# Four shared banks in place of three and one, and the two heads' exponentials of a half pair made in the same step

## The chip, the cores and the metric

The kernel runs on one core of a Trainium2 chip. The metric is the device time of one execution in microseconds, from the program's first instruction to its last; a measurement is the median of several executions. A core has four engines that compute here: TensorE (PE in the profile, with its weight loads as PEld), VectorE (DVE), ScalarE (ACT) and GpSimd (POOL). Each works through its own instruction stream in order. SyncE (SP) issues most of the DMAs, also in order. Results of matmuls land in PSUM, which has eight banks of 2 KB a partition.

## What is computed

Linear attention with exponential features for 8 batches of 8 heads, then a mixer block over the attention's output: a token-mixing MLP and a channel-mixing MLP.

```python
def phi(x):                                   # x: (8, 8, 576, 64), w_phi: (64, 128)
    proj = einsum('bhsd,df->bhsf', x, w_phi)
    proj = proj - max(abs(proj), axis=-1)
    return concatenate([exp(proj), exp(-proj)], axis=-1)
q_p, k_p = phi(q), phi(k)
kv  = einsum('bhsf,bhsd->bhfd', k_p, v);  z = sum(k_p, axis=2)
x   = einsum('bhsf,bhfd->bhsd', q_p, kv) / (einsum('bhsf,bhf->bhs', q_p, z) + 1e-6)
x   = x.transpose(0, 2, 1, 3).reshape(8, 576, 512)
u   = x + (relu(x.T @ w_tok1) @ w_tok2).T     # w_tok1: (576, 256), w_tok2: (256, 576)
out = u + relu(u @ w_ch1) @ w_ch2             # w_ch1: (512, 1536), w_ch2: (1536, 512)
```

## The kernel before

Heads are worked on in pairs: 32 pairs, `i` from 0 to 31, four to a batch. Most products are made of three matmuls of 32-bit halves (`mm3`, line 87): a high and a low part of each operand, without the product of the two low parts.

Five Python generators write the program: `keys`, `queries`, `token_stream`, `load_weights` and `channel_stream`. `weave` advances whichever is furthest behind its share. That gives each instruction a priority. A scheduler then sets the real order of every engine, from its own estimates, and it gives a tile one of the buffers of its tag as that tag has one free. So a change of a tag or of a due step reorders all engines, and only the built order shows how.

**Keys** (line 283). For each pair `load` fetches `raw`, whose single buffer holds the keys of pair i and the queries of pair i-1; `stack` splits them (`stk`, `stq`). `less_max` (line 221) makes scores in five groups: matmuls into a bank (`ppk`), ACT copies one half out (`part`), DVE adds the other half (which frees the bank) and takes the largest magnitude, and POOL subtracts it (`pmk`). ACT makes the exponentials `kp` and `add_kv` adds to `pkv`.

**Queries** (line 350) go in pieces `(i, k, j)`: pair, half of the sequence, and half of that half's rows. `less_max` makes `ppq` and `pmq`. For pairs from 8 on, `across` sends both pieces of a half through memory and back so that they come back turned: DVE transposes into `tq`, one DMA `dq` writes it, four DMAs `qt` read it. What comes back is sorted by head, and from there `j` is the head. A piece waits in the list `waiting` with a due step; from that step on `turn` (line 420) makes that head's exponentials, two signs each: ACT writes `qf` and `qh`, then DVE (first sign) or POOL (second sign) writes `ql = qf - qh`. Each of the tags `qf`, `qh` and `ql` has two buffers, one for each sign, so the exponentials of the next piece can only be written when the matmuls of the one before have read theirs. A one-column copy by POOL (line 445) that the next `qh` begins with shows that moment: POOL waits there for PE. `numerators` (line 504) makes the six matmuls `pn` of one head; ACT and DVE empty that bank and DVE and POOL divide.

**Token mixing** (line 541) begins when a half batch is attended: transposes `px`, a split into `xh` and `xl`, matmuls into `pa`, a relu split into `ah` and `al`, matmuls into `ph`, and DVE's addition to `xt` (line 586). For batch 0 its banks are those of the tags `a0` and `a1`, later those of `rest`.

**Channel mixing** (line 590) takes 18 blocks of 256 tokens, `channel_mix(i)`. It alternates six up-projections, `h{i}_0` to `h{i}_5` of 24 matmuls each, with down-projections `acc`. All `h` share one bank (except in the last three blocks, where odd ones take another), so the next up-projection begins when ACT has written `gh` and DVE `gl` from the one before (lines 617 and 618). The next block begins when the batches under it have been mixed.

The eight PSUM banks: one `keys`, three `rest`, one `kv`, one `h`, and `a0` and `a1`. `rest` serves query scores, transposes, numerators and, from batch 1 on, token mixing. Lines that the change touches: 59, 233, 236, 389 and 608.

Of the kernel before, what the change touches and what calls it, by code (L numbers as in the profile page):

```python
# [8 lines left out]
F32 = mybir.dt.float32  # L9
# [8 lines left out]
P = 128  # L18
B, H, S, D = 8, 8, 576, 64
NP = H // 2  # L20
F = 128
# [14 lines left out]
BEHIND = 2  # L36
TURNED = 4
CH = 256
# [9 lines left out]
def mixer_kernel(ctx, tc, qk, vm, vt, w_phi, w1, w2, wc1, wc2d, out):  # L48
# [5 lines left out]
    ps_w = ctx.enter_context(tc.tile_pool(name="ps_w", bufs=1, space=PSUM))  # L54
# [1 line left out]
    ps_h = ctx.enter_context(tc.tile_pool(name="ps_h", bufs=1, space=PSUM))  # L56
    ps_a = ctx.enter_context(tc.tile_pool(name="ps_a", bufs=1, space=PSUM))

    REST = dict(tag="rest", bufs=3)

    def streamed(pool, shape, dtype, **kw):

# [158 lines left out]
    def less_max(ts, units, name, base=None, early=False):  # L221

        n, kind = len(units), name[0]
        if early and base == D:
            ps = ps_a.tile([P, 2, 2, F], F32, tag=f"a{nplain['k'] % 2}", name=f"pp{name}")
            nplain["k"] += 1
        elif early and base == 0 and (nplain["q"] % 2 == 0 or nplain["q"] >= BORROWED):
            ps = ps_h.tile([P, 2, 2, F], F32, tag="h", name=f"pp{name}")  # L230
            nplain["q"] += 1
        elif early and base == 0:
            ps = ps_w.tile([P, 2, 2, F], F32, tag="keys", name=f"pp{name}", bufs=1)
            nplain["q"] += 1
        elif kind == "k":
            ps = ps_w.tile([P, 2, 2, F], F32, tag="keys", name=f"pp{name}", bufs=1)
        else:
            ps = ps_w.tile([P, 2, 2, F], F32, name=f"pp{name}", **REST)
        for i, u in enumerate(units):
            t, c = (ts[1], 512) if u is None else (ts[u[0]], P * u[1])  # L240
            if base is None:
                nc.tensor.matmul(ps[:, i].rearrange("p two f -> p (two f)"), t[:, c:c + P],  # L242
                                 wp2.rearrange("p two f -> p (two f)"), start=True, stop=True)
            else:
                rows = slice(D, P) if name == "k0_0" else slice(0, P)
                nc.tensor.matmul(ps[:, i, 0], t[rows, c:c + P], wz[rows, base // D], start=True, stop=True)  # L246
        if base is None:
            part = wk.tile([P, 2, F], F32, tag="part", name=f"part{name}")
            nc.scalar.copy(part[:, :n], ps[:, :n, 1])
            pr = wk.tile([P, 2, F], F32, tag="p", name=f"p{name}")  # L250
            nc.vector.tensor_tensor(pr[:, :n], ps[:, :n, 0], part[:, :n], op=ALU.add)
            pr, eng = pr[:, :n], nc.gpsimd
        else:
            pr, eng = ps[:, :n, 0], nc.vector
        mx = column(wk, 2, tag=f"mx{kind}", name=f"mx{name}")
        nc.vector.tensor_reduce(mx[:, :n], pr, axis=AX.X, op=ALU.max, apply_absolute_value=True)  # L256
        pm = wk.tile([P, 2, F], F32, tag=f"pm{kind}", name=f"pm{name}", bufs=1 if kind == "t" else 2)
        eng.tensor_tensor(pm[:, :n], pr, mx[:, :n].unsqueeze(2).to_broadcast([P, n, F]), op=ALU.subtract)  # L258
        return pm
# [90 lines left out]
    def queries():  # L350
        waiting, split_up, row_major, pm = [], [], [], None
        pieces = [(i, k, j) for i in range(B * NP) for k in range(2) for j in range(2)]
        n = 0
        while n < len(pieces) or waiting or split_up or row_major:
            for done in row_major:
                flip(*done)
                yield 0.2
            row_major = []
            for work in split_up:
                yield from until(lambda: work[0] in kvs)  # L360
                if work[0] < ROWS:
                    row_major += [done for done in (row_numerators(*work),) if done]
                else:
                    numerators(*work)
                yield 0.75
            split_up = []
            while waiting and len(split_up) < 2 and (waiting[0][0] <= n or n >= len(pieces)):
                due, work = waiting.pop(0)
                split_up.append(turn(*work, pm if via(work[0]) and n < len(pieces) else None))
                yield 0.02 if via(work[0]) else 0.25  # L370
            if n < len(pieces):
                i, k, j = pieces[n]
                if (k, j) == (0, 0):
                    plain = 0 if i < PLAIN else None
                    if i < PLAIN:
                        yield from until(lambda: i in pairs)
                        ts = pairs[i]
                    else:
                        yield from until(lambda: i + 1 in raws or i + 1 == B * NP)
                        if i + 1 == B * NP:  # L380
                            load(i + 1)
                        ts = stack(raws[i + 1], 0, f"q{i}")
                    asked.add(i)
                    tail = less_max(ts, [None], f"t{i}", plain, i < NP)
                    yield 0.11
                pm = less_max(ts, [(j, 2 * k), (j, 2 * k + 1)], f"q{i}_{k}{j}", plain, i < NP)
                if via(i):
                    across(i, k, j, pm, tail)
                waiting.append((n + 1 + BEHIND * via(i), (i, k, j, pm, tail)))
                yield 0.22  # L390
            n += 1

# [2 lines left out]
    def via(i):  # L395
        return i >= ROWS and i % NP < TURNED
# [23 lines left out]
    def turn(i, k, j, pm, tail, behind):  # L420
# [3 lines left out]
        else:  # L424
            ptr = ps_w.tile([P, 3, P], F32, **REST, name=f"pt{i}_{k}{j}")
            rows = [pm[:, 0], pm[:, 1]]
# [31 lines left out]
    def row_numerators(i, k, j, qps):  # L458
# [6 lines left out]
        if j == 0:  # L465
            sums[0] = ps_w.tile([P, 2, 3, D + 1], F32, **REST, name=f"pr{i}_{k}")
        pn = sums[0]
# [122 lines left out]
    def channel_mix(i, segs):  # L590
        uh, ul = [], []
        for c in range(NC_):
            h = streamed(wk, [P, CH], F32R, tag=f"uh{c}", name=f"uh{i}_{c}", bufs=1)
# [11 lines left out]

        def up_proj(ep):
            if i >= LAST and ep % 2:
                ph = ps_w.tile([P, 2, CH], F32, tag="keys", name=f"h{i}_{ep}", bufs=1)
            else:
                ph = ps_h.tile([P, 2, CH], F32, tag="h", name=f"h{i}_{ep}")  # L610
            for k in range(2):
                es = slice((2 * ep + k) * P, (2 * ep + k + 1) * P)
                for c in range(NC_):
                    mm3(ph[:, k], (wc1_h[:, c, es], wc1_l[:, c, es]), (uh[c], ul[c]), c == 0, c == NC_ - 1)
            gh = streamed(wk, [P, 2, CH], F32R, tag="g", name=f"gh{i}_{ep}", bufs=4)
            gl = streamed(wk, [P, 2, CH], F32R, tag="g", name=f"gl{i}_{ep}", bufs=4)
            nc.scalar.activation(gh, ph, AF.Relu)  # L617
            nc.vector.scalar_tensor_tensor(gl, ph, 0.0, gh.bitcast(F32), op0=ALU.max, op1=ALU.subtract)  # L618
            return gh, gl
# [119 lines left out]
```

## Time and profile before

| | |
|---|---|
| median of 3 executions | 1119.68 us (1118.68 to 1120.17) |
| the profiled execution: its own time | 1120.8 us |
| the profiled execution: span, first to last instruction | 1119.0 us |
| TensorE busy | 1092.4 us of the span |
| TensorE weight loads busy | 1073.2 us |
| VectorE / ScalarE / GpSimd busy | 708.9 / 556.1 / 567.0 us |
| mean granted TensorE clock | 0.995 of full |

Busy time is the time in which an engine had an instruction under way. Matmuls overlap and their ends are modelled, so the time between the starts of two matmuls is the better measure of how fast PE goes. Idle time of an engine is put down to whatever ended it.

### The profile page before, as it was taken

The page shows a single profiled execution, that of the slowest core. Times are in us where ns is not written, and L with a number is a line of the kernel's source. Part 1 is how long each engine was busy: PE and PEld are TensorE (multiplying, and loading weights), DVE is VectorE, ACT ScalarE, POOL GpSimd, SP SyncE. Part 2 cuts the span into 40 slices and gives each one's busy share as a digit, 9 for nine tenths or more (in the row PEclk, how much of TensorE's full clock was granted, in tenths as well). Part 3 has the DMA queues.
Part 4 walks back from the last instruction along what each step waited for, and adds up shares of the span by engine and source line. Part 5 has one row for each costly group of instructions (what it writes and reads, how often), then busy time and mean ns, then how long its engine had stood idle before and what let it go on. Part 6 is the DMA issues. An engine that isn't in the chain of part 4 may idle for free.

```text
span 1119.0 us, 24637 instructions
## 1 busy us (share of the span) xinstructions
PE 1092.4 (98%) x9040; PEld 1073.2 (96%) x9040; DVE 708.9 (63%) x1775; ACT 556.1 (50%) x1589; POOL 567.0 (51%) x1047
## 2 busy tenths in 40 slices
PE   9999999999999999999999999999999989999998
PEld 8998999989998899999999999999999989999998
DVE  6889964467667676767666575764776776642111
ACT  4766553345546464656545464454565656441110
POOL 2334342367647665766656484663675766430110
PEclk9999999999999999999999999999999999999999
DMA  8545401133313232333323232122332232200000
GB/s 204 170 135 151 133 28 52 34 94 78 87 30 92 74 76 71 85 84 75 74 60 80 57 95 69 53 66 70 76 75 63 75 85 45 62 21 20 20 20 19
DMA packets 186744, 82.73 MB, mean 74 GB/s; under 512 B 159424, under 2 KB 171200, under 8 KB 186624
## 3 DMA queue, kind: packets, MB, share of 16 engines
q1 hardware_dynamic: 185104, 80.74, 27.9%
q8 instruction: 71, 1.16, 0.4%
q10 hardware_dynamic: 1520, 0.43, 0.2%
q14 instruction: 49, 0.40, 0.1%
HBM read 57.54 MB, written 23.59 MB: 73 GB/s over the span
## 4 chain that ended last, share of the span: by engine, by line
PE 77%; DVE 9%; POOL 4%; DMA 3%; ACT 3%; issue 2%; SPq 1%; ACTq 0%; POOLq 0%; DVEq 0%
PE h L87 24%; PE acc L87 23%; PE pkv L327 8%; PE pn L87 6%; PE ph L87 4%; PE pa L87 4%; PE pr L472 2%; PE ppk L242 2%; PE ppq L242 2%; DMA raw<-in_qk 1%; PE px L551 1%; DMA v<-in_vm 1%; PE ppq L246 1%; POOL pmq L258 1%; DMA qt<-dq 1%
## 5 line engine op out<-in xcount | busy, mean ns | idle before, releaser
L87 PE MATMUL acc<-gh,wc 128*128 128x256 f32 x1728 | 337.6, 282 | 0.0
L87 PEld LDWEIGHTS acc<-gh,wc 128*128 128x128 f32 x1728 | 273.6, 188 | 0.2
L87 PE MATMUL h<-uh,wc_h 128*128 128x256 f32 x864 | 244.1, 283 | 3.5 <-DVE gl L618 3.1
L87 PE MATMUL h<-uh,wc_l 128*128 128x256 f32 x864 | 244.1, 283 | 0.0
L87 PE MATMUL h<-ul,wc_h 128*128 128x256 f32 x864 | 242.9, 281 | 0.8 <-POOL ul L598 0.8
L87 PE MATMUL acc<-gl,wc 128*128 128x256 f32 x864 | 239.8, 281 | 0.0
L87 PEld LDWEIGHTS h<-uh,wc_h 128*128 128x128 f32 x864 | 162.5, 188 | 5.5 <-PE pn L87 2.8
L87 PEld LDWEIGHTS h<-ul,wc_h 128*128 128x128 f32 x864 | 162.7, 188 | 1.2 <-POOL ul L598 1.0
L87 PEld LDWEIGHTS acc<-gl,wc 128*128 128x128 f32 x864 | 162.5, 188 | 0.0
L87 PEld LDWEIGHTS h<-uh,wc_l 128*128 128x128 f32 x864 | 162.5, 188 | 0.0
L327 PE MATMUL pkv<-v,kp 128*128 128x65 f32 (+2 forms) x1152 | 160.2, 270 | 1.8 <-ACT kp L302 0.7
L327 PEld LDWEIGHTS pkv<-v,kp 128*128 128x128 f32 x1152 | 150.5, 192 | 3.5 <-ACT kp L302 1.6
L302 ACT ACTIVATE kp<-pmk 128x256 f32<-128x256 f32 (+1 forms) x320 | 108.5, 389 | 67.1 <-POOL pmk L258 43.9
L618 DVE SCALAR_TENSOR_TENSOR gl<-h,gh 128x512 fp32r<-128x512 f32 x108 | 73.5, 680 | 98.2 <-ACT gh L617 95.0
L447 POOL TENSOR_TENSOR ql<-qf,qh 128x320 fp32r<-128x320 f32 (+1 forms) x96 | 80.1, 834 | 72.4 <-ACT qh L446 72.1
L617 ACT ACTIVATE gh<-h 128x512 fp32r<-128x512 f32 x108 | 64.4, 596 | 101.1 <-PE h L87 99.4
L438 ACT ACTIVATE qf<-qt 128x320 f32<-128x320 f32 (+1 forms) x192 | 81.6, 437 | 63.0 <-POOL qf L437 29.0
L87 PE MATMUL pn<-qh,kv 128*128 128x320 f32 (+1 forms) x384 | 106.6, 308 | 3.8 <-ACT qh L446 1.6
L598 POOL TENSOR_TENSOR ul<-xt,uh 128x64 fp32r<-128x64 f32 (+3 forms) x120 | 60.6, 530 | 92.3 <-ACT uh L597 92.3
L446 ACT ACTIVATE qh<-qt 128x320 fp32r<-128x320 f32 (+1 forms) x192 | 82.9, 436 | 29.1 <-POOL qh L445 27.0
L217 POOL TENSOR_TENSOR stk<-raw,stk 64x512 fp32r<-64x512 f32 (+1 forms) x48 | 68.3, 1422 | 47.7 <-DVE stk L216 45.2
L258 POOL TENSOR_TENSOR pmk<-pk,mxk 128x256 f32<-128x256 f32 (+1 forms) x120 | 72.8, 606 | 36.0 <-DVE mxk L256 27.8
(129 smaller groups left out, 2293.1 us busy)
## 6 DMA issues: line engine op xcount, KB each, us to landing
raw<-in_qk SPq DMA_DIRECT2D x23, 576.0 KB, 4.2
rawc<-in_wc SPq DMA_DIRECT2D x24, 512.0 KB, 4.1
v<-in_vm SPq DMA_DIRECT2D x31, 256.0 KB, 4.1
dq<-tq SPq DMA_DIRECT2D x24, 320.0 KB, 2.1
qt<-dq SPq DMA_DIRECT2D x96, 80.0 KB, 2.9
dq<-tq SPq DMA_DIRECT2D x24, 256.0 KB, 2.0
qt<-dq SPq DMA_DIRECT2D x96, 64.0 KB, 2.9
out_x<-xt SPq DMA_DIRECT2D x12, 256.0 KB, 2.1
```

The source lines that it names most:

```text
L87: nc.tensor.matmul(o, a, m, start=first and i == 0, stop=last and i == 2, skip_group_check=group_ok)
L217: nc.gpsimd.tensor_tensor(t[lo:lo + D], src, t[base:base + D].bitcast(F32), op=ALU.subtract)
L242: nc.tensor.matmul(ps[:, i].rearrange("p two f -> p (two f)"), t[:, c:c + P], wp2.rearrange("p two f -> p (two f)"), start=True, stop=True)
L258: eng.tensor_tensor(pm[:, :n], pr, mx[:, :n].unsqueeze(2).to_broadcast([P, n, F]), op=ALU.subtract)
L302: nc.scalar.activation(kp[:, :len(us), sg], pm[:, :len(us)], AF.Exp, scale=1.0 - 2.0 * sg)
L327: nc.tensor.matmul(o, kp[:, n, sg], v, start=g == 0 and n == 0 and sg == 0, stop=u is None, skip_group_check=True)
L438: nc.scalar.activation(full, src, AF.Exp, scale=1.0 - 2.0 * sg)
L446: nc.scalar.activation(hi, src, AF.Exp, scale=1.0 - 2.0 * sg)
L447: (nc.gpsimd if sg else nc.vector).tensor_tensor(lo, full, hi.bitcast(F32), op=ALU.subtract)
L598: nc.gpsimd.tensor_tensor(l[:, d:d + n], t[:, c, o:o + n], h[:, d:d + n].bitcast(F32), op=ALU.subtract)
L617: nc.scalar.activation(gh, ph, AF.Relu)
L618: nc.vector.scalar_tensor_tensor(gl, ph, 0.0, gh.bitcast(F32), op0=ALU.max, op1=ALU.subtract)
```

## The change

The tag `keys` goes; what used it takes a buffer of `rest`, which now has four. And the due step of a turned piece depends on `j`: the second piece keeps its step, the first comes one step later, so that both are due in the same one.

```diff
-    REST = dict(tag="rest", bufs=3)
+    REST = dict(tag="rest", bufs=4)
...
         elif early and base == 0:
-            ps = ps_w.tile([P, 2, 2, F], F32, tag="keys", name=f"pp{name}", bufs=1)
+            ps = ps_w.tile([P, 2, 2, F], F32, name=f"pp{name}", **REST)
             nplain["q"] += 1
         elif kind == "k":
-            ps = ps_w.tile([P, 2, 2, F], F32, tag="keys", name=f"pp{name}", bufs=1)
+            ps = ps_w.tile([P, 2, 2, F], F32, name=f"pp{name}", **REST)
...
-                waiting.append((n + 1 + BEHIND * via(i), (i, k, j, pm, tail)))
+                waiting.append((n + 1 + (BEHIND + 1 - j) * via(i), (i, k, j, pm, tail)))
...
             if i >= LAST and ep % 2:
-                ph = ps_w.tile([P, 2, CH], F32, tag="keys", name=f"h{i}_{ep}", bufs=1)
+                ph = ps_w.tile([P, 2, CH], F32, name=f"h{i}_{ep}", **REST)
```

`BEHIND` is 2, and `via(i)` is true for pairs from 8 on. No instruction that computes is added or removed: the built order has the same 8154 matmuls. What moves is shown at three places. In these rows the line of the kernel comes first, then the operation, and the tiles written and read.

The first place is PE at the end of the last half of pair 11, as token mixing of batch 2 begins. `pn11_10` are the numerators of the first head, `pn11_11` those of the second. Before:

```order
L87 MATMUL pn11_10_5105<-ql11_101_5067,kv0_11_4505 128x256
L87 MATMUL pn11_10_5105<-qh11_101_5066,kv1_11_4508 128x256
L87 MATMUL pn11_11_5194<-qh11_110_5154,kv0_11_4505 128x256
L551 MATMUL px2_1_0_5209<-ident_86,xt0_2_3161 128x128 x2
L87 MATMUL pn11_11_5194<-ql11_110_5155,kv0_11_4505 128x256
L87 MATMUL pn11_11_5194<-qh11_110_5154,kv1_11_4508 128x256
```

After:

```order
L87 MATMUL pn11_10_5185<-qh11_100_5128,kv1_11_4490 128x256
L87 MATMUL pn11_10_5185<-qh11_101_5136,kv0_11_4487 128x256
L87 MATMUL pn11_10_5185<-ql11_101_5137,kv0_11_4487 128x256
L87 MATMUL pn11_10_5185<-qh11_101_5136,kv1_11_4490 128x256
L87 MATMUL pn11_11_5198<-qh11_110_5144,kv0_11_4487 128x256
L551 MATMUL px2_1_0_5213<-ident_86,xt0_2_3356 128x128 x2
L87 MATMUL pn11_11_5198<-ql11_110_5145,kv0_11_4487 128x256
```

Before, the first sign of the first head was finished long ahead of the first matmul of `pn11_11`; now three matmuls stand between. Over the 48 half pairs that go this way and both signs, the median number of matmuls between a buffer's last reader of the first head and its first reader of the second was 40 and is 26; the fewest were 13, 16 and 17, and are 3, 3, 5, 5, 7 and 7.

The second place is PE between the first and the second up-projection of block 4. Before:

```order
L87 MATMUL h4_0_5594<-uh4_3_5586,wc1_l_107 128x256
L242 MATMUL ppq13_01_5504<-wp2_91,stq131_5421 128x256 x2
L87 MATMUL pn12_10_5538<-qh12_100_5491,kv0_12_5009 128x256
L242 MATMUL ppq13_10_5623<-wp2_91,stq130_5418 128x256 x2
L87 MATMUL pn12_10_5538<-ql12_100_5492,kv0_12_5009 128x256
L87 MATMUL pn12_10_5538<-qh12_100_5491,kv1_12_5012 128x256
L87 MATMUL pn12_10_5538<-qh12_101_5499,kv0_12_5009 128x256
L87 MATMUL pn12_10_5538<-ql12_101_5500,kv0_12_5009 128x256
L87 MATMUL pn12_10_5538<-qh12_101_5499,kv1_12_5012 128x256
L87 MATMUL acc4_0_5592<-gh4_0_5619,wc2_0_696 128x256
L87 MATMUL acc4_1_5593<-gh4_0_5619,wc2_0_696 128x256
L87 MATMUL h4_1_5668<-uh4_0_5568,wc1_h_106 128x256
```

After:

```order
L87 MATMUL h4_0_5621<-uh4_3_5613,wc1_h_106 128x256
L87 MATMUL h4_0_5621<-ul4_3_5614,wc1_h_106 128x256
L87 MATMUL h4_0_5621<-uh4_3_5613,wc1_l_107 128x256
L87 MATMUL acc4_0_5619<-gh4_0_5646,wc2_0_696 128x256
L87 MATMUL acc4_1_5620<-gh4_0_5646,wc2_0_696 128x256
L87 MATMUL h4_1_5654<-uh4_0_5595,wc1_h_106 128x256
```

The twelve matmuls that stood between the two are two; the ten others stand earlier. Over blocks 0 to 14 the smallest such counts were 10, 11, 11, 12, 12, 12, 13, 14, 15, 15, 15 and 17, and are 2, 4, 4, 6, 8, 10, 13, 14, 15, 16, 19 and 19.

The third place is SP's queue, at the load `raw17`. Before:

```order
L413 DMA dq14_1_6264<-tq14_1_6122 128x512
L417 DMA qt14_1_6266<-dq14_1_6264 32x16x32
L269 DMA raw17_7003<-in_qk 128x1152
L417 DMA qt14_1_6266<-dq14_1_6264 32x16x32
L293 DMA v1_113<-in_vm 128x8x64
```

After:

```order
L413 DMA dq14_1_6266<-tq14_1_6112 128x512
L269 DMA raw17_6993<-in_qk 128x1152
L293 DMA v1_113<-in_vm 128x8x64
L417 DMA qt14_1_6268<-dq14_1_6266 32x16x32 x4
```

The load stood behind the first `qt`, which waits for `dq` to land, and now stands ahead of it. Of the 22 loads of `raw` from pair 11 on, 2 stood ahead of all four `qt` and now 11 do.

## Rows read from the trace of the kernel before

**Rows 1.** The page: span, and busy time of each engine.

```profile
span 1119.0 us, 24637 instructions
PE 1092.4 (98%) x9040; PEld 1073.2 (96%) x9040; DVE 708.9 (63%) x1775; ACT 556.1 (50%) x1589; POOL 567.0 (51%) x1047
```

**Rows 2.** Busy time by stretch: from:to, length, PE (matmuls), PEld, DVE, ACT, POOL, clock, DMA.

```profile
336.00:392.00 56.00, 50.96 (x389) 48.29 (x389) 41.51 (x103) 31.70 (x98) 40.39 (x78) 0.97 0.33 81
...
560.00:896.00 336.00, 333.52 (x2788) 330.55 (x2787) 224.00 (x558) 178.83 (x524) 203.77 (x395) 1.00 0.28 70
896.00:952.00 56.00, 53.38 (x443) 52.42 (x442) 39.48 (x103) 34.48 (x103) 37.13 (x73) 1.00 0.27 65
...
1064.00:1119.00 55.00, 50.95 (x436) 50.74 (x434) 8.99 (x13) 6.67 (x13) 2.85 (x4) 1.00 0.06 20
```

**Rows 3.** Waits of PE: us in total, times, longest us.

```profile
PE h L87 <- DVE gl L618: 3.1, 5, 1.0
...
PE pn L87 <- ACT qh L446: 1.6, 2, 1.2
...
PE pn L87 <- DVE xt L586: 1.2, 1, 1.2
...
PE pn L87 <- DVE den L520: 0.7, 2, 0.4
PE ppk L242 <- DVE pk L251: 0.7, 2, 0.4
...
PE pa L87 <- DVE den L520: 0.4, 1, 0.4
PE px L551 <- DVE den L520: 0.4, 2, 0.2
```

**Rows 4.** Waits of POOL, ACT and DVE, same columns.

```profile
ACT qf L438 <- DMA qt<-dq: 19.6, 11, 3.6
...
POOL qh L445 <- PE pn L87: 17.7, 25, 2.4
...
DVE stk L216 <- DMA raw<-in_qk: 15.7, 8, 4.0
```

**Rows 5.** Timeline of PE, second place (block 4): start, us, engine, instruction, idle before.

```profile
379.77 0.28 PE L87 MATMUL h<-uh,wc_l 128*128 128x256 f32 x1
...
381.05 0.40 PE L87 MATMUL acc<-gh,wc 128*128 128x256 f32 x2
382.13 0.35 PE L87 MATMUL h<-uh,wc_h 128*128 128x256 f32 x1 [0.68 <-DVE gl L618]
```

**Rows 6.** Timelines of ACT and DVE at the same place.

```profile
380.08 0.60 ACT L617 ACTIVATE gh<-h 128x512 fp32r<-128x512 f32 x1 [0.70 <-PE h L87]
...
380.66 0.72 DVE L216 CAST stq<-raw 64x512 fp32r<-64x512 f32 x1 [0.51 <-PE ppq L242]
381.31 0.67 DVE L618 SCALAR_TENSOR_TENSOR gl<-h,gh 128x512 fp32r<-128x512 f32 x1
```

**Rows 7.** PE, POOL, ACT, DVE: from head 0's matmul to head 1's exponentials, pair 17.

```profile
522.12 0.39 PE L87 MATMUL pn<-qh,kv 128*128 128x320 f32 x1
...
524.34 0.30 POOL L445 CAST qh<-pmq 128x1 fp32r<-128x1 f32 x2
...
524.55 0.47 ACT L446 ACTIVATE qh<-qt 128x320 fp32r<-128x320 f32 x1 [0.80 <-POOL qh L445]
...
525.05 0.49 DVE L447 TENSOR_TENSOR ql<-qf,qh 128x320 fp32r<-128x320 f32 x1 [0.47 <-ACT qh L446]
```

**Rows 8.** PE, ACT, DVE: the same steps at pair 31.

```profile
989.57 0.28 PE L87 MATMUL pn<-qh,kv 128*128 128x256 f32 x1
...
990.58 0.40 ACT L446 ACTIVATE qh<-qt 128x256 fp32r<-128x256 f32 x1
...
991.15 0.42 DVE L447 TENSOR_TENSOR ql<-qf,qh 128x256 fp32r<-128x256 f32 x1
```

**Rows 9.** Busy time in a stretch at a lower clock, columns as in Rows 2.

```profile
368.60:372.00 3.40, 3.40 (x16) 3.40 (x17) 0.88 (x3) 0.95 (x4) 1.13 (x2) 0.51 0.83 224
```

## Prediction, made before the changed kernel was run

> **What bounds the kernel now.** I read the page first: PE is busy for 1092.4 of 1119.0 us, and no other engine passes 709 [rows 1]. No matmul is added or removed, so what the change can give or take is PE's idle time, 26.6 us in all, and the clock. Next I read the busy time by stretch, to see where the idle time lies. From 560 to 896 us PE idles for 2.5 us in 336; from 336 to 392 it idles for 5.0 in 56, from 896 to 952 for 2.6 in 56, and 4.1 lie in the last 55 us, after the attention work and out of the change's reach [rows 2]. So the kernel has long stretches that are full, where an earlier result is worth nothing, and short ones where PE has too little to choose from: there a batch's last numerators, its token mixing and the first up-projections of the next block follow each other, each waiting for ACT, DVE or POOL to hand the last one's result on. Then I read PE's waits one by one, for what ends them [rows 3]. The largest entry, 3.1 us in five waits, is an up-projection that waits for `gl` of the one before.
>
> Where PE does not wait, one matmul follows the other every 0.116 us: at the second place of the order 11 steps lie between 379.77 and 381.05 [rows 5]. I use that as the price of a matmul.
>
> **The change part by part.**
>
> *Four shared banks instead of three and one.* No instruction changes its length; what can go is a wait for a bank. PE's waits that ended on the reader of such a bank are 0.7 us for the single `keys` bank (`pk` had to empty it), and 1.2, 0.7, 0.4 and 0.4 us where numerators, `pa` or `px` waited for a bank of `rest` that `xt` or `den` had yet to empty [rows 3]. They are 3.4 us. The first 0.7 I count whole, since a second bank was never there for keys; of the other 2.7 half, since the fourth buffer is now wanted by keys too: -2.0 us. Bounds: 0, if keys fill the ring as fast as it grows, and -3.4.
>
> The Trainium skill, Perfetto Trace Analysis, section Optimization Strategy, says that the same gap repeating on the engine that should be saturated can mean that there isn't enough PSUM for the next tile. By that rule the change would be worth the whole 3.4 us, 1116.3 us; the trace agrees only in part, since the gap that repeats most (3.1 us in five waits) is for `h`, whose bank the change leaves alone [rows 3].
>
> *The first head's exponentials a step later.* They can start later relative to the transposed data, and `raw` is now often loaded ahead of the four `qt` instead of behind one or all. ACT waited 19.6 us in 11 waits for `qt`, and DVE 15.7 us in 8 for `raw` [rows 4]. Both are in-order engines, so what stood behind came late too. But PE was fed meanwhile: a wait of these engines hurts only in the short stretches. I take -1.0 us; bounds 0 and -3, about the idle time of one such stretch [rows 2].
>
> *The two heads close together.* The cost of putting both heads in one step is a loop that closes on itself: PE's third matmul of the first head sets `qh` free, POOL's one-column copy follows, ACT writes `qh`, DVE or POOL writes `ql`, and PE begins the second head. POOL already waits for PE at this point, 25 times [rows 4]. The trace shows how long the loop takes. At pair 17 the matmul ends at 522.51, POOL's copy begins at 524.34, `qh` ends at 525.02 and `ql` at 525.54: 2.51 and 3.03 us after the end [rows 7]. At pair 31, where nothing stands ahead on these engines and POOL's copy is absent, `qh` ends 1.13 us and `ql` 1.72 us after the matmul's end [rows 8]. With the matmul's own 0.28 us, PE reaches the next head too early unless (n + 1) x 0.116 us is more than 1.41 us, n being the matmuls between.
>
> Before, the fewest were 13. Now two places have 3 and two have 7 for one of their signs (the second sign at the first two, with 5, runs its loop while PE waits for the first). That costs 2 x (1.41 - 0.46) + 2 x (1.41 - 0.93) = 2.9 us with the quick loop, and with pair 17's, which begins with a matmul of 0.39 us, 2 x (2.90 - 0.46) + 2 x (2.90 - 0.93) = 8.8 us. I take the quick one, because at these places PE idles and the others have little in front, as at pair 31. The wait of 1.6 us that PE had for `qh` [rows 3] is this loop at work in the old order; it is replaced, so I take it off: net +1.3 us, bounds 0 and +7.2. At all other half pairs the median is 26 matmuls, 27 x 0.116 = 3.1 us of work, which hides a loop of 2.90 us as at pair 17, though not by much; before it was 40 matmuls or 4.8 us.
>
> *The second up-projection of a block comes sooner.* At block 4 the last matmul of the first up-projection starts at 379.77. ACT starts `gh` 0.31 us later and needs 0.60, `gl` takes 0.67, and the next up-projection starts 0.15 us after `gl`'s end [rows 5, 6]. That is 1.73 us at the least; here it was 2.36, because DVE was first busy with `stq` [rows 6]. Twelve matmuls hid most of it and PE idled for 0.68 us [rows 5]. With two matmuls between, the least idle time is 1.73 - 3 x 0.116 = 1.38 us. Over the twelve smallest counts the least is 1.38 + 2 x 1.15 + 0.92 + 0.69 + 0.45 + 0.11 = 5.9 us after, and 0.45 + 2 x 0.34 + 3 x 0.22 + 0.11 = 1.9 before, where the trace has 3.1. I take the difference, +4.0 us. With 2.36 us for every one of the twelve the sum after would be 11.8, which bounds it at +8.7. The lower bound is 0: the ten matmuls that left this place stand earlier now, and may fill a wait there that is just as long.
>
> *The rest.* In the last three blocks odd up-projections get more banks; PE has hardly an idle moment there up to the last stretch [rows 2], and the up-projections hide it: nothing. The clock: in the stretch from 368.6 us, inside one of the starved ones, it was granted at 0.51, and 16 matmuls went where 3.40 / 0.116 = 29 would have: 1.5 us lost [rows 9]. That is the lower of its two levels, 1.2 GHz. One such stretch more or fewer is 1.5 us either way; I put it in the range alone.
>
> Sum: -2.0 - 1.0 + 1.3 + 4.0 = +2.3 us. The profiled execution took 1120.8 us, 1.8 more than its span; by it the sum gives 1123.1. It is 1.1 over the median of the runs, 1119.7, from which I predict 1122.0 us.
>
> **The rivals.** A: *the banks and the loads win.* The idle time at the up-projections only moves (0 instead of +4.0) and the loop is hidden (0 for it, and the 1.6 us of old waits gone). With the banks at their bound it is -3.4 - 1.0 - 1.6 = -6.0 us, 1113.7 us. For it speaks that all of PE's large waits lie in few places, so that matmuls moved there are worth their full time; against it, that after the change less stands at the up-projections than the chain there needs in any case.
>
> B: *the loop becomes the rule.* It decides from the point where the loop takes more than the 3.1 us that 26 matmuls give; then not four but most of the 48 half pairs wait, and each further 0.1 us costs up to 4.8 us. Pair 17's loop, at 2.90, is short of it by 0.2 us. For it speaks that POOL took 1.83 us to come to a one-column copy there [rows 7]; against it, that the loop took 1.41 us where nothing was in front [rows 8]. With the long loop at the tight places alone it is -2.0 - 1.0 + 7.2 + 4.0 = +8.2, 1127.9 us; with 0.1 us at every half pair, 1132.7.
>
> C: *nothing moves the end.* Gains and losses lie in the full stretches and are hidden; 1119.7 us.
>
> **How the numbers follow.** About 0.2%, 2.2 us, is what a measurement of this kernel can tell from no change: faster means below 1117.4, slower above 1121.9. To the forecast (losses a little larger than gains, 1118 to 1125) I give 0.35, to A 0.28, to B 0.25, to C 0.12. The forecast's own range straddles the bound: 0.03 of it faster, 0.16 same, 0.16 slower. A is faster but for 0.01, B slower, C the same. Together: faster 0.30, same 0.29, slower 0.41. The range for 8 in 10 runs from A's side, 1113, to B's with half of its spread, 1130.
>
> **What would show it.** In the profile after: PE's wait for `gl` should be 5 to 9 us instead of 3.1, and its wait for `qh` and `ql` 2 to 4 us, with gaps of about 1 us at the last halves of pairs 11 and 27. The wait of 0.7 us that ended on `pk` at a score's matmul should be gone, and DVE's wait for `raw` and ACT's for `qt` should be shorter. If the wait for `gl` stays near 3 us, the fourth step is wrong; if waits for `qh` appear in the full stretches, B is right. The prediction as a whole is wrong if the starved stretches get longer or shorter as a whole, which the orders do not tell, or if the number of stretches at the low clock changes.

## Result, and the profile after

The changed kernel took 1129.15 us (median of 3, 1128.54 to 1131.54) against 1119.68 before: a ratio of 1.0086, 95% interval 1.0072 to 1.0101, or 9.5 us slower. The profiled execution has a span of 1129.6 us against 1119.0, so 10.6 us are to be found in the two traces.

The page of the changed kernel, span and busy time of each engine (answers to [rows 1]):

```profile
span 1129.6 us, 24532 instructions
PE 1097.2 (97%) x9040; PEld 1076.5 (95%) x9040; DVE 718.8 (64%) x1775; ACT 563.7 (50%) x1589; POOL 568.4 (50%) x1043
```

PE idles for 32.4 us instead of 26.6. That is only 5.8 of the 10.6: matmuls overlap, and a PE that is short of work is also busy for longer with each. The number of matmuls in a stretch says more. (The count takes in those under way at an end of the stretch, so neighbours share two or three.) Busy time by stretch after (answers to [rows 2], same columns; the last row is again the last 55 us):

```profile
336.00:392.00 56.00, 49.34 (x370) 46.13 (x369) 45.19 (x109) 33.82 (x103) 41.24 (x80) 0.97 0.34 84
560.00:896.00 336.00, 333.12 (x2780) 330.67 (x2780) 225.20 (x551) 179.77 (x522) 204.26 (x395) 1.00 0.29 72
896.00:952.00 56.00, 53.13 (x424) 51.56 (x424) 41.22 (x103) 32.50 (x95) 36.45 (x71) 0.98 0.23 61
1074.60:1129.60 55.00, 51.00 (x434) 50.79 (x432) 8.99 (x13) 6.70 (x13) 2.85 (x4) 1.00 0.06 20
```

The two starved stretches have 19 matmuls fewer each, the full one between them 8. To see the whole I cut the span into other stretches and read PE alone (from:to, length, busy, matmuls, clock, DMA). Before:

```profile
0.00:120.00 120.00, 114.23 (x912) 1.00 0.59 166
120.00:320.00 200.00, 196.12 (x1634) 0.99 0.24 64
320.00:400.00 80.00, 74.96 (x594) 0.98 0.31 75
...
480.00:520.00 40.00, 38.40 (x303) 0.96 0.30 75
520.00:880.00 360.00, 358.18 (x3003) 1.00 0.29 72
880.00:920.00 40.00, 36.73 (x295) 1.00 0.30 74
920.00:1060.00 140.00, 139.44 (x1179) 1.00 0.14 36
```

After:

```profile
0.00:120.00 120.00, 110.90 (x860) 0.99 0.58 162
120.00:320.00 200.00, 198.75 (x1680) 1.00 0.25 66
320.00:400.00 80.00, 73.34 (x574) 0.98 0.30 74
...
480.00:520.00 40.00, 35.57 (x274) 1.00 0.31 78
520.00:880.00 360.00, 358.39 (x3010) 1.00 0.28 71
880.00:920.00 40.00, 35.86 (x264) 0.96 0.30 75
920.00:1060.00 140.00, 139.10 (x1167) 1.00 0.16 38
```

At 0.116 us each, the missing matmuls are 52 in the first 120 us (6.0 us), 20, 29 and 31 in the three starved stretches (2.3, 3.4 and 3.6), and 12 from 920 to 1060 (1.4); 46 and 7 more stand from 120 to 320 and from 520 to 880 (-5.3 and -0.8). From 400 to 480 us both have 671. The sum is 91 matmuls, 10.6 us, to within the two or three that neighbours share. So there are two losses, one at the very start, where plain pairs run, and one where batches end; and there is a gain between them, which leaves the change only 6 matmuls behind at 320 us. Some 11 matmuls of that first loss and 14 of the gain are a place at the lower clock, which stands at 113.0 us now (18 matmuls in 3.40 us, where 29 would have gone) and stood at 235.5 before (15).

Waits of PE after (answers to [rows 3]; us in total, times, longest):

```profile
PE h L87 <- DVE gl L618: 3.4, 6, 1.2
PE pn L87 <- ACT qh L446: 3.2, 2, 2.9
...
PE acc L87 <- ACT gh L617: 1.9, 4, 0.7
PE ppt L242 <- DVE xl L81: 1.6, 3, 0.7
PE pn L87 <- DVE ql L447: 1.5, 2, 0.9
...
PE pr L472 <- DVE dn L487: 1.1, 1, 1.1
...
PE acc L87 <- DVE gl L618: 0.7, 1, 0.7
PE pn L87 <- POOL ql L447: 0.7, 2, 0.3
```

The waits for a bank in [rows 3] have no counterpart any more: a key's score that waited for `pk`, and numerators, `pa` and `px` that waited for `xt` or `den`. They were 3.4 us. But others have come in their place. `ppt`, the scores of a sequence's last rows, wait 1.6 us for `xl` to empty a bank of the ring, `ppq` 0.3 us for `xt`, and `pr`, the numerators of a plain pair, 1.1 us. (`pr` reads `kv` and `qf`, which ScalarE writes, so its wait for VectorE's `dn` is one for a bank.) Together they are 3.0 us. Waits of POOL and ACT after (answers to [rows 4]):

```profile
POOL qh L445 <- PE pn L87: 59.3, 64, 2.8
...
ACT qf L438 <- DMA qt<-dq: 7.5, 2, 4.0
```

GpSimd's one-column copy waits for TensorE 64 times instead of 25; ScalarE waits for `qt` twice instead of 11 times, and VectorE's row for `raw` is gone.

The worst place is the last half of pair 11. PE there, after (timeline: start, us, instruction, idle time before it):

```profile
353.06 0.39 PE L242 MATMUL ppk<-wp,stk 128*128 128x256 f32 x2
356.32 0.39 PE L87 MATMUL pn<-qh,kv 128*128 128x256 f32 x1 [2.87 <-ACT qh L446]
357.35 0.39 PE L87 MATMUL pn<-ql,kv 128*128 128x256 f32 x1 [0.64 <-DVE ql L447]
...
358.50 0.94 PE L87 MATMUL pn<-qh,kv 128*128 128x256 f32 x2
```

and GpSimd and ScalarE at that time:

```profile
354.00 1.26 POOL L217 TENSOR_TENSOR stq<-raw,stq 64x512 fp32r<-64x512 f32 x1
355.32 0.18 POOL L437 COPY qf<-pmq 128x1 f32<-128x1 f32 x1
...
355.01 0.37 ACT L519 COPY xt<-pn 64x256 f32<-64x256 f32 x1 [0.42 <-DVE den L520]
355.54 0.42 ACT L438 ACTIVATE qf<-qt 128x256 f32<-128x256 f32 x1 [0.17 <-POOL qf L437]
```

The 2.87 us are not the loop between the two heads, since it is the first head that waits; the second head's first matmul is the later one of the two at 358.50, and waits for nothing. The first head's exponentials are late on every engine: the copies of the step stand on GpSimd behind `pmk`, `pmq` and 1.26 us of `stq`; ScalarE waits 0.17 us for them, after 0.42 us in which it waited for VectorE's `den`; and PE has nothing left. At pair 27 the larger gap is the first head's too:

```profile
891.61 0.27 PE L87 MATMUL pn<-qh,kv 128*128 128x256 f32 x1
892.78 0.39 PE L87 MATMUL pn<-ql,kv 128*128 128x256 f32 x1 [0.90 <-DVE ql L447]
...
894.26 0.39 PE L87 MATMUL pn<-qh,kv 128*128 128x256 f32 x1 [0.38 <-ACT qh L446]
```

The six numerators of a head read `qh`, `ql`, `qh`, `qh`, `ql` and `qh`. So the 0.90 us stand between the first two of the first head, while VectorE was busy with additions of channel mixing's `xt` up to 891.93 us and wrote `ql` after them. The loop between the heads is the 0.38 us at 894.26, where the second head begins.

The clock is at the lower level in three places again, though not the same ones (the column of the clock is under 1 in the first stretch and the one from 880 us now, and no longer from 120 and from 480 us). One of them, with 14 matmuls where [rows 9] has 16:

```profile
358.80:362.20 3.40, 3.34 (x14) 3.14 (x15) 1.98 (x4) 2.10 (x8) 1.58 (x3) 0.51 0.45 72
```

### The profile page after: what moved, and what is told of

It is laid out like the page before. It is cut to its first block, busy times and chain, and to the rows that moved or that the text cites. A ratio compares the mean times of both kernels' runs of the same rounds, so it can differ in the third digit from the quotient of the medians.

```text
span 1129.6 us, 24532 instructions
## 1 busy us (share of the span) xinstructions
PE 1097.2 (97%) x9040; PEld 1076.5 (95%) x9040; DVE 718.8 (64%) x1775; ACT 563.7 (50%) x1589; POOL 568.4 (50%) x1043
## 4 chain that ended last, share of the span: by engine, by line
PE 81%; DVE 10%; POOL 4%; ACT 2%; issue 2%; DMA 1%; SPq 0%; POOLq 0%; ACTq 0%; DVEq 0%
PE h L87 25%; PE acc L87 24%; PE pkv L327 8%; PE pn L87 6%; PE ph L87 4%; PE pa L87 3%; PE ppk L242 2%; PE pr L472 2%; PE ppq L242 2%; PE px L551 1%; PE ppk L246 1%; PE ppq L246 1%; PE pt L430 1%; POOL pmq L258 1%; DVE bitsc L153 1%
## 5 line engine op out<-in xcount | busy, mean ns | idle before, releaser
L327 PE MATMUL pkv<-v,kp 128*128 128x65 f32 (+2 forms) x1152 | 154.2, 272 | 1.7 <-ACT kp L302 1.2
L327 PEld LDWEIGHTS pkv<-v,kp 128*128 128x128 f32 x1152 | 144.5, 192 | 3.2 <-ACT kp L302 1.4
L598 POOL TENSOR_TENSOR ul<-xt,uh 128x64 fp32r<-128x64 f32 (+3 forms) x120 | 65.0, 568 | 78.5 <-ACT uh L597 77.1
L447 DVE TENSOR_TENSOR ql<-qf,qh 128x320 fp32r<-128x320 f32 (+1 forms) x96 | 54.5, 567 | 62.4 <-ACT qh L446 61.9
```

The costliest lines, as they stand in the source:

```text
L327: nc.tensor.matmul(o, kp[:, n, sg], v, start=g == 0 and n == 0 and sg == 0, stop=u is None, skip_group_check=True)
L447: (nc.gpsimd if sg else nc.vector).tensor_tensor(lo, full, hi.bitcast(F32), op=ALU.subtract)
L598: nc.gpsimd.tensor_tensor(l[:, d:d + n], t[:, c, o:o + n], h[:, d:d + n].bitcast(F32), op=ALU.subtract)
```

## Experiments

Each kernel was timed in five rounds beside the kernel before, whose median was 1119.25 to 1119.57. The table gives the difference of the medians, the interval of the ratio, and from the profile of each the matmuls of PE in some stretches; the column 120–1060 is the sum of the seven stretches in it. (The change and the first row for before are the three executions above.)

| kernel | us | difference | ratio, 95% | 0–120 | 120–1060 | 320–400 | 480–520 | 880–920 |
|---|---|---|---|---|---|---|---|---|
| before | 1119.68 | | | 912 | 7679 | 594 | 303 | 295 |
| the change | 1129.15 | +9.5 | 1.0072–1.0101 | 860 | 7640 | 574 | 274 | 264 |
| ring alone | 1126.07 | +6.8 | 1.0043–1.0074 | 866 | 7681 | 619 | 300 | 292 |
| step alone | 1127.94 | +8.7 | 1.0058–1.0091 | 916 | 7618 | 566 | 269 | 291 |
| both heads later | 1133.69 | +14.4 | 1.0111–1.0151 | 913 | 7566 | 534 | 309 | 295 |
| share 0.23 | 1119.45 | +0.2 | 0.9991–1.0011 | 918 | 7684 | 597 | 296 | 297 |
| second head sooner | 1144.86 | +25.3 | 1.0215–1.0249 | 918 | 7467 | 595 | 209 | 263 |
| ring, early share 0.30 | 1133.08 | +13.5 | 1.0103–1.0133 | 872 | 7602 | 606 | 300 | 316 |
| before, early share 0.30 | 1118.65 | -0.9 | 0.9985–1.0002 | 917 | 7682 | 624 | 309 | 294 |
| ring, scores on `h` | 1128.89 | +9.3 | 1.0068–1.0093 | 850 | 7672 | 616 | 298 | 290 |
| step but for last pairs | 1136.75 | +17.2 | 1.0136–1.0165 | 910 | 7540 | 608 | 241 | 239 |
| step for last pairs only | 1125.02 | +5.5 | 1.0035–1.0062 | 917 | 7633 | 565 | 302 | 293 |
| before, scores on `h` | 1120.59 | +1.1 | 1.0001–1.0027 | 883 | 7695 | 596 | 308 | 295 |
| the change without a copy | 1125.88 | +6.3 | 1.0041–1.0065 | 852 | 7695 | 598 | 280 | 298 |

Two things help to read it. Kernels whose PE has the same order in the first 120 us differ there by 8 matmuls (910 to 918, the old banks with any due step) and by 14 (852 to 866, the ring with either due step or without the copy): so much is noise. And the mean granted clock of the profiled executions is 0.986 to 0.989 in five of them (step alone, both heads later, second head sooner, ring with early share 0.30, step but for last pairs) and 0.994 to 0.998 in all others, the change included. Against the 0.995 of before that is 0.006 to 0.009 of some 1130 us, or 7 to 10 us of full-speed time: an upper estimate of what the clock costs these five, since PE idled for a part of it.

**The ring alone.** The change without its last line, the due step.

```diff
-    REST = dict(tag="rest", bufs=3)
+    REST = dict(tag="rest", bufs=4)
...
-            ps = ps_w.tile([P, 2, 2, F], F32, tag="keys", name=f"pp{name}", bufs=1)
+            ps = ps_w.tile([P, 2, 2, F], F32, name=f"pp{name}", **REST)
```

> The ring of four alone, with the old due step. Lost time of PE (steps between matmuls over the nominal step, by 40 us) grew after the change by 5.5 us in the first 120 us, where the plain pairs' scores now take a bank of the ring, by 2.3 from 320 to 400, 3.3 from 480 to 520 and 3.5 from 880 to 920. Theory R (the shared ring costs, at the start): +4 to +5.5 us, 1124 to 1125, and the first 120 us show it while the later stretches stand as before. Theory S (the due step costs, where batches end): 0 to -2 us, 1118 to 1120, and the first 120 us hardly move, or what they lose is given back later. Theory O (any new order moves the time by some us): no relation to either, within 5 us of before.

Theory R is right that the ring costs, and that it costs at the start: 46 matmuls or 5.3 us in the first 120 us. The time is beyond its range (6.8 us against 4 to 5.5), and the later stretches do not stand as before. From 120 us on the ring is worth nothing either way, 7681 matmuls against 7679, but only as a balance: from 120 to 400 us it has 56 more, and from 520 to 880 us, which no theory named, 46 fewer, with numerators waiting for `qh` 2.5 us in 4 instead of 0.4 in 1. PE by stretch, ring alone:

```profile
0.00:120.00 120.00, 110.82 (x866) 0.99 0.58 163
520.00:880.00 360.00, 355.76 (x2957) 1.00 0.29 71
```

What PE waits for in the first 120 us is mostly data. Matmuls by line in that time, before (busy, mean ns, idle before and what ended it):

```profile
L327 PE MATMUL pkv<-v,kp 128*128 128x128 f32 (+1 forms) x224 | 30.9, 276 | 0.4 <-ACT kv L336 0.2
L472 PE MATMUL pr<-kv,qf 128*128 128x65 f32 (+1 forms) x200 | 24.7, 262 | 0.6 <-ACT qf L438 0.3 <-ACT kv L336 0.2
```

and with the ring alone:

```profile
L327 PE MATMUL pkv<-v,kp 128*128 128x128 f32 (+1 forms) x216 | 30.3, 282 | 2.2 <-ACT kp L302 2.2
L472 PE MATMUL pr<-kv,qf 128*128 128x65 f32 (+1 forms) x200 | 25.0, 261 | 1.6 <-DVE dn L487 1.1 <-ACT kv L336 0.5
```

The 1.1 us of `pr` are a wait for a bank, as in the change. The 2.2 us are one wait for `kp`. On ScalarE these exponentials stood behind a weight's conversion that waited 2.71 us for its DMA:

```profile
27.68 0.49 ACT L150 ACTIVATE bits<-raw 128x320 f32<-128x320 f32 x1 [2.71 <-DMA raw<-in_w]
28.07 0.71 ACT L302 ACTIVATE kp<-pmk 128x256 f32<-128x256 f32 x2
```

Before, that conversion (128x320) came at 28.70 us, behind three `kp`, and waited for nothing. Another 13 of the 46 matmuls went at the lower clock: from 112.6 to 116.0 us 19 matmuls are under way at 0.50, where before has 32 at full clock.

**The step alone.** Before's banks and the new due step.

```diff
-                waiting.append((n + 1 + BEHIND * via(i), (i, k, j, pm, tail)))
+                waiting.append((n + 1 + (BEHIND + 1 - j) * via(i), (i, k, j, pm, tail)))
```

> The due step alone, with three banks of the ring and one for keys. The fewest matmuls in the loop of the two heads are 4, 5 and 7 and at most half pairs 28. Theory S: +5 us or more, 1124 to 1128, as waits for qh, ql, gl and gh of 4 us more at the batches' ends, and the first 120 us as before, since plain pairs have no second due step. Theory R: at most +1 us, 1120. Theory O: no relation, within 5 us. If parts add up, this and the ring alone give +9.5 together.

Theory S holds beside R, in its time and its places: the first 120 us are untouched, and 320 to 400 and 480 to 520 us lose 28 and 34 matmuls. The parts don't add up: 6.8 and 8.7 alone, 9.5 together. Much of the loss here is the clock, which stayed low for longer in the starved stretches (0.94 and 0.91 against 0.98 and 0.96 before); the mean over the span, 0.989 against 0.995, puts it at 6.8 us at most:

```profile
320.00:400.00 80.00, 73.44 (x566) 0.94 0.29 72
...
480.00:520.00 40.00, 36.48 (x269) 0.91 0.28 68
```

Here, unlike in the change, it is the second head of pair 11 that waits longest, 0.47 us for `qh` and then for `ql`:

```profile
358.85 0.58 PE L87 MATMUL pn<-ql,kv 128*128 128x256 f32 x1 [2.10 <-DVE ql L447]
```

**Both heads later.**

```diff
-BEHIND = 2
+BEHIND = 3
```

> The old banks; both heads of a half pair come one step later, still one step apart. The loop of the two heads has a median of 53 matmuls (40 before, 26 in the change). Two forms of theory S part here. S1 (it costs because the heads are close together, the loop of qh closes): 1119.7, within 2 us. S2 (it costs because the exponentials come later, so that a batch's last numerators come later and the mixing behind them too): +3 to +5 us, 1123 to 1125, with the loss at 340 to 400 and 880 to 920. Theory O: no relation.

S1 falls as the only cause: the heads stand no closer than before, and the kernel is 14.4 us slower. S2 had the direction, not the size (3 to 5 us), and one of its two places: 320 to 400 us lost 60 matmuls, at a clock of 0.89, but 880 to 920 us none (295), and 56 were lost from 600 to 640 us, where pair 19 ends a batch, at a clock of 0.91:

```profile
600.00:640.00 40.00, 37.38 (x284) 36.50 (x283) 23.17 (x55) 18.89 (x55) 20.79 (x35) 0.91 0.26 67
```

**Another share.** The last `yield 0.22` of `queries` becomes 0.23.

> The kernel before with one number changed that has nothing to do with banks or due steps: the share that a query piece counts for is 0.23 instead of 0.22, so that the generators are interleaved a little otherwise and much of the order of every engine is another. Theories R and S: 1119.7 within 1.5 us. Theory O: 2 to 5 us from before, either way; then a difference of a few us says little about the edit that brought it.

Theory O falls for the old banks and the stretches after the start: much of the order is another, and the time is the same. It says less of the start, where the order stays the same for the first 650 matmuls, and nothing of the ring, for which see below.

**The second head sooner.**

```diff
-                waiting.append((n + 1 + BEHIND * via(i), (i, k, j, pm, tail)))
+                waiting.append((n + 1 + (BEHIND - j) * via(i), (i, k, j, pm, tail)))
```

> The old banks; the two heads of a half pair in one step, as in the change, but the second comes a step sooner instead of the first a step later. The loop of the two heads is as short as in the step alone (median 28 matmuls, fewest 3, 3, 3, 5, 5, 5). The step alone took +8.7 us and both heads a step later +14.4. S1 (closeness costs): +5 to +9, 1124 to 1128. S2 (lateness costs): within 2 us of before, 1117 to 1121, with 585 matmuls or more from 320 to 400 us (594 before, 566 with the step alone, 534 with both later) and low-clock stretches no longer than the 10.2 us of before.

S2 falls too, by the largest loss of all, which is far beyond the range of S1 as well. At the end of pair 15, from 480 to 520 us, PE had 209 matmuls at a mean clock of 0.83, and it waited for one thing after the other:

```profile
485.25 0.47 PE L242 MATMUL ppk<-wp,stk 128*128 128x256 f32 x2 [1.76 <-DVE pk L251]
...
486.78 0.58 PE L87 MATMUL pn<-ql,kv 128*128 128x256 f32 x1 [0.94 <-DVE ql L447]
...
489.90 0.58 PE L87 MATMUL pn<-qh,kv 128*128 128x256 f32 x1 [1.69 <-ACT qh L446]
```

Later, sooner and closer all cost: the two heads at their old steps were the best of the four spacings tried.

**The ring with another early order, and its partner.** In both, a plain piece's exponentials count for 0.30 instead of 0.25.

```diff
-                yield 0.02 if via(work[0]) else 0.25
+                yield 0.02 if via(work[0]) else 0.3
```

> The ring of four with the old due step, and another order of the early part: the share counted for a plain piece's exponentials is 0.30 instead of 0.25. The ring alone took +6.8 us and reached 866 matmuls in the first 120 us, before 912. R1 (the shared ring itself holds up the plain pairs): 860 to 880 matmuls in 120 us and 1124 to 1127. R2 (that early order was unlucky: exponentials of keys that stood on ScalarE behind a wait for a weight's DMA, 2.7 us at 27.7 us): 890 to 915 matmuls and 1119 to 1122.

> The kernel before with the same other share of a plain piece, 0.30 instead of 0.25, as the partner of the run above. R1: 905 to 918 matmuls in the first 120 us and 1119.3 within 1.5 us. R2: any early order may lose some us, so 870 to 915 matmuls and 1119 to 1124.

For the start R1 holds and R2 falls: with four shared banks 872 matmuls, with the old banks 917, in orders that differ from those of the other two kernels. The time is outside both ranges, 1133.08 us. The ring lost a further 79 matmuls after 120 us in this order, more than either theory expected. A part of it is the clock (0.98 and 0.96 from 120 to 320 and 320 to 400 us, where the ring alone has 1.00 and 0.98); the rest was not looked into further. The two ring kernels differ in the order alone and are some 7 us apart, the two with the old banks 0.9: for the ring an order alone can move the time, as theory O said, and a difference of some us between two kernels with the ring says little about the edit.

**Plain query scores on one bank, with the ring and without it.**

```diff
-        elif early and base == 0 and (nplain["q"] % 2 == 0 or nplain["q"] >= BORROWED):
+        elif early and base == 0:
```

> The ring of four with the old due step, but the plain pairs' query scores all use the bank of h, so that early the ring serves transposes and numerators alone. R1, if the cost comes from scores and numerators in one ring: 895 to 915 matmuls in the first 120 us, 1119 to 1121, unless the one bank for scores costs as much, which would show as waits of PE for pmq there. R2: no reason for either; anything from 860 to 910.

> The old banks, but all plain query scores in the bank of h, so that the bank of keys stands empty while the plain pairs run; the partner of the ring with these scores on h, which reached 850 matmuls in the first 120 us at +9.3 us. R3 (plain query scores need a second bank that they share with nobody; the ring takes it away): 850 to 875 matmuls here too, and 1124 to 1129. R4 (a fourth bank for transposes and numerators is itself what lets the order go wrong): 905 to 918 matmuls, 1118 to 1121.

The edit reaches less far than the expectations say: line 229 asks for `early`, which is true for the first four pairs alone. From pair 4 on the scores of queries use `rest` in both kernels, and those of keys use their own bank in the one and the ring in the other. And all forecasts of matmuls were missed: 850 with the ring, below both ranges, and 883 with the old banks, between the two; of the times R4's alone held, 1120.59 us. So neither R3 nor R4 is the whole. Taking the second bank away from these scores costs 29 matmuls early (912 to 883) and 1.1 us in the end. With these scores kept out of the ring, 33 more are missing with it (883 to 850) and 8.3 us lost (1120.59 to 1128.89). So the larger part does not come from the first pairs' query scores. Whether it comes from a fourth bank for what used `rest` before, from the keys' scores that share it from pair 4 on, or from the order that follows, no run here tells apart. The Trainium skill, Perfetto Trace Analysis, section Optimization Strategy, says that the same gap repeating on the engine that should be saturated can mean too little PSUM for the next tile. The runs do not bear that out here: with one bank more, shared, for the tiles that had waited, the kernel was slower, and waits for a bank came back at other tiles.

**The step by place.** The late step for all pairs but each batch's last, and for the last alone.

```diff
-                waiting.append((n + 1 + BEHIND * via(i), (i, k, j, pm, tail)))
+                late = 1 - j if i % NP < NP - 1 else 0
+                waiting.append((n + 1 + (BEHIND + late) * via(i), (i, k, j, pm, tail)))
...
+                late = 1 - j if i % NP == NP - 1 else 0
```

> The old banks; the new due step for all turned pairs but the last of each batch (pairs 11, 15, 19, 23, 27, 31), which keep the old one. The step for all pairs took +8.7 us, and its PE lost 3.3 us more from 320 to 400 and 4.0 more from 480 to 520, where pairs 11 and 15 end a batch. S3 (the cost is made where a batch ends, by its own last pair coming late): at most +2 us, 1118 to 1122, with 590 and 300 matmuls in those stretches as before (594 and 303). S4 (the order of the whole, with the work that is left to fill the end, decides): +4 to +9 us, 1123 to 1128.

> The complement: the new due step for the last pair of each batch alone. S3: +5 to +9 us, 1124 to 1128, with fewer than 580 matmuls from 320 to 400 us and fewer than 285 from 480 to 520. S4: 0 to +4 us, 1119 to 1123.

At pair 11 S3 is right: with the last pair late there are 565 matmuls from 320 to 400 us, with the last pair on time 608. At pairs 15 and 27 it is wrong: there the last pair late costs nothing (302 and 293), and a last pair on its old step behind pairs on the new one costs most (241 and 239, at clocks of 0.91 and 0.87). S4 fares no better in its times: 17.2 us where it allowed 9, and 5.5 where it allowed 4. What the two runs leave standing is that the cost is not made by the last pair's lateness alone: it depends on how the last pieces of a batch are spaced against those before.

**The change without GpSimd's copy ahead of `qh`.**

```diff
-            if behind is not None:
-                nc.gpsimd.tensor_copy(hi[:, :1], behind[:, 0, :1])
```

> The changed kernel without GpSimd's one-column copy ahead of qh, so that ScalarE itself waits for TensorE to be done with the buffer, and what stands behind the copy on GpSimd (pmk, pmq, ql) does not. GpSimd waited 59.3 us in 64 waits there after the change (17.7 in 25 before), ScalarE 40.6 us for the copy. L (the loop through this queue costs): 3 to 5 us less than the changed kernel, 1124 to 1126. M (the loop is not what costs; TensorE's own waits for qh and ql at pairs other than the last of a batch are under 1 us): within 2 us of 1129, or slower, since ScalarE's kp now stand behind the wait.

L's time holds: 3.3 us less than the change. From 120 us on this kernel has 7695 matmuls, 16 more than before and 55 more than the change, most of them from 320 to 400 and from 880 to 920 us. What is left of the loss lies in the first 120 us, 852 against 912. PE's waits for `qh` and `ql` fell from 5.4 us to 2.2. But the largest that is left, 1.88 us, is again the first head's of pair 11, so what the copies hold up is less the loop between the heads than the queue as a whole; and PE's order is another one from its 1367th matmul on, so that copy and order are not told apart.

## Why the prediction was right or wrong

The direction and the range held; the time was 7 us too low. That the direction came out is luck for a good part: the two terms that were to win time lost it, and of the two that were to lose time one did so at another place than its mechanism says. The range held the time because rival B had stretched it to 1130.

*Four shared banks, -2.0.* This step failed. The waits on which it rested did go, 3.4 us, but 3.0 us of others for a bank of the same ring came, and the ring alone costs 6.8 us. I had costed the waits that it removes and not the places where it adds some: the first 120 us, where plain pairs use these banks and where 46 to 52 matmuls are missing, and with the ring alone 520 to 880 us, where 46 are. The bounds of 0 to -3.4 excluded a loss because I looked for a bank that is short. What got longer at the start are a wait for a bank, `pr`'s, and waits for data, `kp` and `pmt`, made by engines that came late, with 3.4 us at the lower clock behind them.

*The first head later, -1.0.* It failed. The waits for `qt` and `raw` shrank as expected, and nothing came of it. Instead the first head itself is late where a batch ends. Its numerators wait 3.83 us for `qh` and `ql` at pair 11 (2.87, 0.64 and 0.32) and 0.90 at pair 27, 4.7 us in all; before, a first head waited 0.44 us, at pair 21.

*The heads close together, +1.3.* This step failed too, though its sign came out. PE's waits for `qh` and `ql` are 5.4 us in 6 instead of 1.9 in 3 (1.6 and one of 0.3), and they stand at the last halves of pairs 11 and 27, as forecast. But the loop would hold up the second head, and second heads wait 0.7 us after (0.38 at pair 27, 0.34 in pair 8), against 1.5 before (1.21 at pair 11, 0.33 at pair 21). The rest are the first heads of the step above. That a second head can be held up the step alone shows, with 2.10 us at one of them. GpSimd's queue, which I named, does cost: without its copy there the change gets 3.3 us back.

*The up-projections sooner, +4.0.* The mechanism is right, and the size 1.1 us too large. Waits for `gl` and `gh`, at up- and down-projections, are 6.0 us in 11 after, against 3.1; 5.0 of them stand at blocks 4, 6, 10, 11 and 13, the five with the fewest matmuls between, for which the working of the forecast gives 5.3. The forecast took the difference from 1.9 us that it had worked out, and not from the 3.1 that the trace had: 5.9 - 3.1 = 2.8 us, where 2.9 were measured. Its sign to look for, a wait for `gl` of 5 to 9 us, was missed all the same (4.1 us), since the matmuls that now come first behind an up-projection are down-projections, which wait for `gh`. And the due step is not needed for such a loss: the ring alone has 5.1 us in 3 waits for `gl`.

*The rest, nothing.* Right: in the last 55 us PE is busy for 51.00 us, before for 50.95. The last three blocks take 107.6 us instead of 104.3 (from the last down-projection of one block to that of the next), of which 3.0 lie in the first of them; 16 more matmuls, of other work, stand in it, and PE idles there for 0.7 us.

*The clock.* It was rightly left out of the sum: three places at the lower level before and three after. In five of the experiments it could not have been.

The rivals: A fell with both its terms. B's long loop did not come, but its time, 1127.9, was nearest. C fell.

What stays open: why the shared ring slows the start, and why the change does not lose from 520 to 880 us what the ring alone loses there. One wait for `kp` was followed to a weight's DMA, which explains 2.2 of 5.3 us in one order; the other orders with the ring lose as much at other places. Why a batch's end suffers from every other spacing was followed at pairs 11 and 27 of the change alone. The step with the old banks and without the copy was not tried; that it would be a little faster than before is a guess from the last run's 16 matmuls.

## What to carry to other kernels

A change of a shared resource is to be costed in every stretch in which it is used, also in those that look like a mere start: here the start lost 52 matmuls, of which the next 200 us gave 46 back. A wait that an edit removes can come back at another tile of the same ring, as 3.0 of 3.4 us did. The end of a batch, where PE has little to choose from, is sensitive to the spacing of the pieces that feed it; a step more or less cost 5 to 25 us, most of it there. Counting matmuls per stretch finds such losses where the sum of idle time shows half of them.

## What the runs showed of the hardware

Starved stretches can cost twice, once in idle time and once in the clock. At 0.51 of the full clock, the lower of the two levels at 1.2 GHz, matmuls follow each other every 0.21 us (896.33, 896.55, 896.76 in the timeline of the change) instead of 0.116. In the run with the second head sooner the stretch from 480 to 520 us was granted 0.83 on average and had 209 matmuls against 303, which is 10.9 us. PE was idle there for 5.3 us more than before; the other half went, in the main, at the lower level. It fell there at 486.4 us, behind waits of 1.76 and 0.94 us, with 1.69 us to follow, and no single wait in the stretch was longer. In the change the clock took nothing extra, with three places at the lower level as before.
